# Layernorm, linear attention and a GELU layer on one core: W1 loaded as row blocks, tile 0 accumulated block by block

## The chip, the cores and the metric

One core of a Trainium2 chip runs the whole kernel in one launch. The metric is the device time of that launch in microseconds; before the change it was 204.91 us (median of 3 runs, 204.80 to 204.93). The profile of the kernel before has a span of 203.5 us from the first to the last instruction. Names: TensorE (PE in the profile, PEld for its weight loads, PEq for its sequencer), VectorE (DVE), ScalarE (ACT), GpSimd (POOL), SyncE (SP, which only issues transfers here).

## The reference, cut to what matters

```python
x = A_x                                   # [1, 2048, 640] bf16
xn = _layernorm(x, axis=-1)               # (x - mean) / sqrt(var + 1e-5)
return x + _A_ref(xn, A_wqkv, A_wo) + _B_ref(xn, B_w1, B_b1, B_w2, B_b2)

def _B_ref(x, w1, b1, w2, b2):            # w1 [640, 1536], w2 [1536, 640]
    h = _gelu(jnp.einsum("bsd,df->bsf", x, w1) + b1)
    return jnp.einsum("bsf,fd->bsd", h, w2) + b2
# _A_ref: linear attention with 32 heads of 20, phi(t) = where(t > 0, t + 1, exp(t)) + 1e-6
```

The change touches the start alone: the layernorm of the first tokens and h for them. The 2048 tokens are 16 tiles (t) of 128. D = 640 is five row blocks of 128 (k, DT = 5), F = 1536 is twelve column blocks of 128 (jb, JT = 12).

## The kernel before

A small planner notes for each instruction what it reads and writes, and puts in the semaphore waits; each engine runs its instructions in the order in which they are written here. `take(n)` gives the next of 8 PSUM banks in a ring. `HW` is half a row, 320 elements.

Loads, in order of issue: x tiles and W1 in three column thirds, of the first third two row blocks on ScalarE's queue.

```python
FW = F // NW1                                     # NW1 = 3, FW = 512
def dma_w1(i, eng="sync"):
    dma_w(eng, W1[:, :, i*FW:(i+1)*FW], w1v[:, :, i*FW:(i+1)*FW], r_W1[i])
KA = 2
dma_x(0, 1)
dma_w("scalar", b1tmp[:], B_b1..., r_b1tmp)
dma_w("scalar", W1[:, 0:KA, 0:FW], w1v[:, 0:KA, 0:FW], r_W1A)
dma_x(1, 1)
dma_w("sync", W1[:, KA:DT, 0:FW], w1v[:, KA:DT, 0:FW], r_W1[0])
dma_w1(1)
dma_x(2, 1)
dma_w1(2)
dma_x(3, 1); dma_x(4, 2); dma_x(6, 2); dma_x(8, 4)
```

Layernorm of a tile: two halves of statistics and their aggregate on VectorE (GpSimd adds eps in between), the power -0.5 on GpSimd, and the normalization on VectorE.

```python
def ln_half(t, h):      # VectorE bn_stats of half h; for h == 0 GpSimd then adds D*EPS
    ...
def ln_aggr(t):
    s = t % 4
    Pl.ins(v, lambda e: e.bn_aggr(aggr[:, s, :], stats[:, s, :]), ...)
    Pl.ins(g, lambda e: e.tensor_tensor(out=rstd[:, s:s+1], in0=aggr[:, s, 1:2],
                                        in1=mhalf[:], op=ALU.pow), ...)
def ln_stats(t): ln_half(t, 0); ln_half(t, 1); ln_aggr(t)
def ln_norm(t):         # VectorE tensor_scalar: (x - mean) * rstd, all 640 columns
    ...
```

h needs x with the feature on the partitions (xnT). Tiles 0 to 2 are transposed by TensorE into PSUM and copied from there, tiles 3 to 15 by a DMA transpose after their normalization. A unit of h is five matmuls and a Gelu:

```python
def h_unit(t0, n, jb):                            # n tiles at once
    b = take(1); w = n * P; tok = slice(t0*P, t0*P + w)
    Pl.ins("tensor", [matmul(bank(b, 0, w), W1[:, k, jb*P:(jb+1)*P], xnT[:, k, tok],
                             start=(k == 0), stop=(k == DT-1)) for k in range(DT)], ...)
    Pl.ins("scalar", ... HG[:, jb, tok] = Gelu(bank(b, 0, w) + b1c[:, jb:jb+1]))
```

The start of the schedule (shortened; `filler(n)` is n matmuls of 512 columns on zeros):

```python
... ScalarE: one Gelu on one column               # loads the Gelu table
filler(6); b1_step(); filler(3)
ln_stats(0); ln_half(1, 0); ln_half(1, 1)
norm_part(0, 0, CA, r_xnA); norm_part(0, CA, D, r_xnB)      # CA = 256 columns
ln_aggr(1)
dA, sA, bA = transp_part(0, 0, 2, r_xnA)
filler(1)
dB, sB, bB = transp_part(0, 2, DT, r_xnB)
... ScalarE copies part A to xnT, VectorE part B
norm_part(1, 0, CA, r_xnA1); norm_part(1, CA, D, r_xnB1)
h_first(0, [0, 1, 2, 3], r_xnTA, {... tile 1's transposes and copies in between})
h_first(1, [0, 1, 2, 3], r_xnTA1)                 # 40 matmuls of 128 columns
units(0, 2, JQ, 2*JQ + 1)                         # JQ = 4: 25 matmuls of 256 columns
ln_stats(2); ln_norm(2); ln_stats(3)
xnT_copy(2, transp(2))                            # VectorE copies tile 2's transposes
units(0, 2, 2*JQ + 1, JT)                         # 15 matmuls of 256 columns
ln_next(3)                    # ln_half(4, 0); ln_norm(3); ln_half(4, 1); ln_aggr(4)
xnT_dma(3)                                        # DMA transpose of tile 3
units(2, 1, 0, 10); units(3, 1, 0, 10); units(2, 2, 10, JT)
for t in range(4, NT): ...                        # layernorm and DMA transpose of the rest
```

Everything after this (the other h units, the attention, the output) is the same in both kernels.

Of the kernel before, what the change touches and what calls it, by code (L numbers as in the profile page):

```python
# [6 lines left out]
ACT = mybir.ActivationFunctionType  # L7
P = 128
FP32 = mybir.dt.float32
BF16 = mybir.dt.bfloat16  # L10
# [102 lines left out]
def bass_parallel_sum__linear_attn_block__dense_activation_gelu__prompt_kernel(  # L113
    nc: bass.Bass, A_x, A_wqkv, A_wo, B_x, B_w1, B_b1, B_w2, B_b2, out):
    Batch, S, D = A_x.shape
# [22 lines left out]
    with contextlib.ExitStack() as es:  # L138
# [59 lines left out]
        def take(n):  # L198
            b = ring[0]
            if n == 2 and b % 2:  # L200
                b += 1
            b %= 8
            ring[0] = (b + n) % 8
            return b

        def bank(b, lo=0, hi=512):
            return ps[:, b * 512 + lo: b * 512 + hi]
# [9 lines left out]
        r_xb = [R_("xb%d" % t) for t in range(NT)]  # L217
        r_xn = [R_("xn%d" % t) for t in range(NT)]
        r_xnT = [R_("xnT%d" % t) for t in range(NT)]
        NW1 = 3  # L220
        r_W1A = R_("W1_0A")
        r_W1 = [R_("W1_%d" % i) for i in range(NW1)]
        r_Wq, r_Wk, r_Wv, r_W2 = R_("Wq"), R_("Wk"), R_("Wv"), R_("W2")
        r_Wo = [R_("Wo%d" % i) for i in range(2)]
        r_oT = [R_("oT%d" % i) for i in range(2 * DT)]
# [31 lines left out]
        def dma_x(t, n):  # L257
            src = xv[t * P:(t + n) * P, :].rearrange("(t p) d -> p t d", p=P)
            Pl.ins("sync", lambda e: e.dma_start(x_in[:, t:t + n, :], src),
                   writes=r_x[t:t + n], dma=True)  # L260

        def dma_w(eng, dst, src, res):
            Pl.ins(eng, lambda e: e.dma_start(dst, src), writes=[res], dma=True)  # L263

        w1v = B_w1.rearrange("(k p) n -> p k n", p=P)
        wqv = A_wqkv.rearrange("(k p) n -> p k n", p=P)
        FW = F // NW1
        def dma_w1(i, eng="sync"):
            dma_w(eng, W1[:, :, i * FW:(i + 1) * FW], w1v[:, :, i * FW:(i + 1) * FW], r_W1[i])
        KA = 2  # L270
        dma_x(0, 1)
        dma_w("scalar", b1tmp[:], B_b1.rearrange("(a p) -> a p", p=P), r_b1tmp)
        dma_w("scalar", W1[:, 0:KA, 0:FW], w1v[:, 0:KA, 0:FW], r_W1A)
        dma_x(1, 1)
        dma_w("sync", W1[:, KA:DT, 0:FW], w1v[:, KA:DT, 0:FW], r_W1[0])
        dma_w1(1)
        dma_x(2, 1)
        dma_w1(2)
        dma_x(3, 1)
        dma_x(4, 2)  # L280
        dma_x(6, 2)
# [40 lines left out]
        def filler(n):  # L322
            b = take(1)
            Pl.ins("tensor", [lambda e: e.matmul(bank(b), warm[:, 0:P], warm[:], start=True, stop=True)
                              for _ in range(n)], reads=[r_warm], writes=[B_[b]])
# [9 lines left out]
        def ln_half(t, h):  # L335
            s = t % 4
            Pl.ins(v, lambda e: e.bn_stats(stats[:, s, 6 * h:6 * h + 6], x_in[:, t, h * HW:(h + 1) * HW]),  # L337
                   reads=[r_x[t]], writes=[r_stats[s][h]])
            if h == 0:
                Pl.ins(g, lambda e: e.tensor_single_scalar(stats[:, s, 2:3], stats[:, s, 2:3], D * EPS, ALU.add),  # L340
                       reads=[r_stats[s][0]], writes=[r_stats[s][0]])

        def ln_aggr(t):
            s = t % 4
            Pl.ins(v, lambda e: e.bn_aggr(aggr[:, s, :], stats[:, s, :]),
                   reads=r_stats[s], writes=[r_aggr[s]])
            Pl.ins(g, lambda e: e.tensor_tensor(out=rstd[:, s:s + 1], in0=aggr[:, s, 1:2],
                                                in1=mhalf[:], op=ALU.pow),
                   reads=[r_aggr[s], r_small], writes=[r_rstd[s]])

        def ln_stats(t):
            ln_half(t, 0)
            ln_half(t, 1)
            ln_aggr(t)
# [22 lines left out]
        def h_unit(t0, n, jb):  # L377
            b = take(1)
            w = n * P
            tok = slice(t0 * P, t0 * P + w)  # L380
            Pl.ins("tensor", [(lambda e, k=k: e.matmul(  # L381
                bank(b, 0, w), W1[:, k, jb * P:(jb + 1) * P], xnT[:, k, tok],
                start=(k == 0), stop=(k == DT - 1))) for k in range(DT)],
                reads=[r_W1[jb * P // FW]] + r_xnT[t0:t0 + n], writes=[B_[b]])
            Pl.ins("scalar", lambda e: e.activation(  # L385
                HG[:, jb, tok], bank(b, 0, w), ACT.Gelu_apprx_tanh, bias=b1c[:, jb:jb + 1]),
                reads=[B_[b], r_b1c], writes=[r_HG[t][jb] for t in range(t0, t0 + n)])


        CA = 2 * P  # L390
        r_xnA, r_xnB = R_("xn0A"), R_("xn0B")

        def norm_part(t, lo, hi, res):
            s = t % 4
            Pl.ins(v, lambda e: e.tensor_scalar(xn_tm[:, t, lo:hi], x_in[:, t, lo:hi], aggr[:, s, 0:1], rstd[:, s:s + 1],
                                                ALU.subtract, ALU.mult),
                   reads=[r_x[t], r_aggr[s], r_rstd[s]], writes=[res, r_xn[t]])

        def transp_part(t, k0, k1, res):
            b = take(1)  # L400
            pT = bank(b).bitcast(BF16)
            Pl.ins("tensor", [(lambda e, k=k: e.transpose(pT[:, (k - k0) * P:(k - k0 + 1) * P],
                                                          xn_tm[:, t, k * P:(k + 1) * P], ident[:]))
                              for k in range(k0, k1)],
                   reads=[res, r_ident], writes=[B_[b]])
            return xnT[:, k0:k1, t * P:(t + 1) * P], pT[:, 0:(k1 - k0) * P].rearrange("p (k q) -> p k q", k=k1 - k0), b

        def h_first(t, jbs, resA, between=None):
            bs = [take(1) for _ in jbs]
            tok = slice(t * P, (t + 1) * P)  # L410
            for (ks, res) in (((0, 1), resA), ((2, 3, 4), r_xnT[t])):
                for i, (jb, b) in enumerate(zip(jbs, bs)):
                    Pl.ins("tensor", [(lambda e, k=k, jb=jb, b=b: e.matmul(
                        bank(b, 0, P), W1[:, k, jb * P:(jb + 1) * P], xnT[:, k, tok],
                        start=(k == 0), stop=(k == DT - 1))) for k in ks],
                        reads=[r_W1A if res is resA else r_W1[jb * P // FW], res], writes=[B_[b]])
                    if between and res is not resA and i in between:
                        between[i]()
            for jb, b in zip(jbs, bs):
                Pl.ins("scalar", lambda e, jb=jb, b=b: e.activation(  # L420
                    HG[:, jb, tok], bank(b, 0, P), ACT.Gelu_apprx_tanh, bias=b1c[:, jb:jb + 1]),
                    reads=[B_[b], r_b1c], writes=[r_HG[t][jb]])

        r_xnTA, r_xnTA1 = R_("xnT0A"), R_("xnT1A")
        r_xnA1, r_xnB1 = R_("xn1A"), R_("xn1B")
        Pl.ins("scalar", lambda e: e.activation(b1c[:, 0:1], warm[:, 0:1], ACT.Gelu_apprx_tanh),
               reads=[r_warm], writes=[r_b1c])
        filler(6)
        b1_step()
        filler(3)  # L430
        ln_stats(0)
        ln_half(1, 0)
        ln_half(1, 1)
        norm_part(0, 0, CA, r_xnA)
        norm_part(0, CA, D, r_xnB)
        ln_aggr(1)
        dA, sA, bA = transp_part(0, 0, 2, r_xnA)
        filler(1)
        dB, sB, bB = transp_part(0, 2, DT, r_xnB)
        Pl.ins("scalar", lambda e: e.activation(dA, sA, ACT.Copy), reads=[B_[bA]], writes=[r_xnTA])  # L440
        Pl.ins(v, lambda e: e.tensor_copy(dB, sB), reads=[B_[bB]], writes=[r_xnT[0]])
        norm_part(1, 0, CA, r_xnA1)
        norm_part(1, CA, D, r_xnB1)

        def copy_part(k0, k1, res, dst):
            d, s, b = transp_part(1, k0, k1, res)
            Pl.ins(v, lambda e: e.tensor_copy(d, s), reads=[B_[b]], writes=[dst])

        h_first(0, [0, 1, 2, 3], r_xnTA, {1: lambda: copy_part(0, 2, r_xnA1, r_xnTA1),
                                          3: lambda: copy_part(2, DT, r_xnB1, r_xnT[1])})  # L450
        h_first(1, [0, 1, 2, 3], r_xnTA1)

        def xnT_dma(t):
            Pl.ins("sync", lambda e: e.dma_start_transpose(xnT[:, :, t * P:(t + 1) * P], xn_tm[:, t, :]),
# [1 line left out]

        late = Pl.records["sync"][x_done:]
        del Pl.records["sync"][x_done:]
        JQ = JT // NW1

        def units(t0, n, lo, hi):
            for jb in range(lo, hi):
                h_unit(t0, n, jb)

        def ln_next(t):
            if t + 1 < NT:
                ln_half(t + 1, 0)
            ln_norm(t)
            if t + 1 < NT:
                ln_half(t + 1, 1)  # L470
                ln_aggr(t + 1)

        units(0, 2, JQ, 2 * JQ + 1)
        ln_stats(2)
        ln_norm(2)
        ln_stats(3)
        xnT_copy(2, transp(2))
        units(0, 2, 2 * JQ + 1, JT)
        ln_next(3)
        xnT_dma(3)  # L480
        units(2, 1, 0, 10)
        units(3, 1, 0, 10)
# [353 lines left out]
```

## Time and profile before

| what | value |
|---|---|
| time, median of 3 | 204.91 us |
| span of the profile | 203.5 us, 3162 instructions |
| granted TensorE clock by the page | 1.00 |
| first row that uses W1 (L413) | starts at 6.45 us |
| tile 2's transposes on TensorE (L365) | start at 12.26 us |
| DMA transpose of tile 3, issue and length in the chain | 14.56 us, 2.66 us |
| first matmul on tile 3 | 17.27 us |
| last matmul ends, by the chain | 201.7 us |

How to read it: the page gives busy time by engine, the span in 40 slices of about 5 us (each digit is tenths of busy), and the chain of work that ended last, followed back from the last instruction. A row of the timeline has start, length, engine, line of the kernel, operation, destination and source, shapes and count, and in brackets how long the engine sat idle before it and what released it; instructions of one kind are merged. Matmuls are pipelined, so a merged length is more than the count times the spacing, and a row of "busy" on TensorE does not mean that it works at its peak. A transfer's time to landing runs from its issue to the semaphore's last step.

### The profile page before, as it was taken

The page shows a single profiled execution, that of the slowest core. Times are in us where ns is not written, and L with a number is a line of the kernel's source. Part 1 is how long each engine was busy: PE and PEld are TensorE (multiplying, and loading weights), DVE is VectorE, ACT ScalarE, POOL GpSimd, SP SyncE. Part 2 cuts the span into 40 slices and gives each one's busy share as a digit, 9 for nine tenths or more (in the row PEclk, how much of TensorE's full clock was granted, in tenths as well). Part 3 has the DMA queues.
Part 4 walks back from the last instruction along what each step waited for, and adds up shares of the span by engine and source line. Part 5 has one row for each costly group of instructions (what it writes and reads, how often), then busy time and mean ns, then how long its engine had stood idle before and what let it go on. Part 6 is the DMA issues. An engine that isn't in the chain of part 4 may idle for free.

```text
span 203.5 us, 3162 instructions
## 1 busy us (share of the span) xinstructions
PE 199.4 (98%) x1153; PEld 106.7 (52%) x1170; DVE 122.1 (60%) x246; ACT 73.6 (36%) x144; POOL 14.4 (7%) x43
## 2 busy tenths in 40 slices
PE   7999999999999999999999999999999999999996
PEld 2789885444444444644456565444444444444444
DVE  4579855000005899999458899595794297348222
ACT  3589886666667555121233596200000000000000
POOL 3136534000000000000000000000000000000000
PEclk9999999999999999999999999999999999999999
DMA  5974996999901111000179934117266926851541
GB/s 154 360 263 98 123 191 120 240 348 221 323 8 29 26 26 26 3 0 0 35 178 373 160 64 98 55 22 161 31 122 195 144 52 115 153 120 31 164 117 52
DMA packets 52550, 25.45 MB, mean 125 GB/s; under 512 B 38119, under 2 KB 52535, under 8 KB 52535
## 3 DMA queue, kind: packets, MB, share of 16 engines
q1 hardware_dynamic: 48782, 23.80, 50.1%
q10 hardware_dynamic: 3752, 1.45, 4.2%
q8 instruction: 9, 0.15, 0.3%
q14 instruction: 7, 0.05, 0.1%
HBM read 12.72 MB, written 2.62 MB: 75 GB/s over the span
## 4 chain that ended last, share of the span: by engine, by line
PE 90%; DMA 5%; DVE 2%; SPq 1%; issue 1%; POOL 0%; DVEq 0%
PE ps L745 29%; PE ps L381 21%; PE ps L584 11%; PE ps L573 8%; PE ps L532 8%; PE ps L710 7%; DMA xPK<-in_A_x_dram 3%; PE ps L563 2%; PE ps L523 2%; DMA xnT<-xn_tm 1%; DVE stats L337 1%; PE ps L598 1%; PE ps L616 1%; SPq L263 0%; DVE xn_tm L358 0%
## 5 line engine op out<-in xcount | busy, mean ns | idle before, releaser
L381 PE MATMUL ps<-xnT,W 128*128 128x256 bf16 (+2 forms) x372 | 50.5, 296 | 0.3
L385 ACT ACTIVATE HG<-ps,b1c 128x256 bf16<-128x256 f32 (+2 forms) x75 | 37.4, 522 | 13.5 <-PE ps L381 11.7
L745 PE MATMUL ps<-HG,W 128*128 128x512 bf16 x188 | 41.9, 379 | 0.2
L381 PEld LDWEIGHTS ps<-xnT,W 128*128 128x128 bf16 x375 | 32.2, 98 | 17.9 <-DMA xnT<-xn_tm 0.3
L745 PEld LDWEIGHTS ps<-HG,W 128*128 128x128 bf16 x192 | 18.8, 98 | 22.6
L584 PE MATMUL ps<-xnT,Wqkv 128*128 128x512 bf16 x97 | 22.4, 379 | 0.2
L745 PE MATMUL ps<-PQ,Msb 128*128 128x512 bf16 x78 | 17.8, 379 | 0.1
L532 PE MATMUL ps<-Wqkv,xnT 128*128 128x512 bf16 x78 | 17.8, 379 | 0.1
L573 PE MATMUL ps<-xPK,xn_tm 128*128 128x512 bf16 x78 | 17.2, 379 | 0.1
L337 DVE BATCH_NORM_STATS2 stats<-xPK 128x6 f32<-128x320 bf16 x32 | 13.7, 468 | 5.7 <-DMA xPK<-in_A_x_dram 5.7
L584 PEld LDWEIGHTS ps<-xnT,Wqkv 128*128 128x128 bf16 x100 | 11.3, 118 | 8.7
L507 ACT ACTIVATE xn_tm<-ps 128x512 bf16<-128x512 f32 x20 | 11.9, 597 | 9.5 <-PE ps L584 8.9
L510 DVE SCALAR_TENSOR_TENSOR PQ<-ps,xn_tm 128x512 bf16<-128x512 f32 x20 | 13.8, 692 | 2.1
L507 ACT ACTIVATE ek<-ps 128x512 bf16<-128x512 f32 x20 | 11.8, 597 | 8.4 <-PE ps L532 6.4
L518 DVE CAST b2c<-out_l 128x5 f32<-128x5 bf16 x1 | 0.2, 172 | 23.2 <-DMA out_l<-b2bc 23.2
L649 DVE TENSOR_REDUCE den_sb<-xn_tm 128x128 f32<-128x512 f32 x4 | 4.1, 1037 | 16.1 <-DMA xn_tm<-xn_tm 16.1
L751 DVE SCALAR_TENSOR_TENSOR W<-ps,b2c,xnT 128x512 bf16<-128x512 f32 x16 | 11.3, 734 | 2.8 <-PE ps L745 2.4
L532 PEld LDWEIGHTS ps<-Wqkv,xnT 128*128 128x128 bf16 x80 | 7.8, 98 | 9.4
L745 PEld LDWEIGHTS ps<-PQ,Msb 128*128 128x128 bf16 x80 | 7.8, 98 | 9.4
L573 PEld LDWEIGHTS ps<-xPK,xn_tm 128*128 128x128 bf16 x80 | 7.8, 98 | 9.3
L633 DVE SCALAR_TENSOR_TENSOR xn_tm<-PQ,z_sb,xn_tm 128x512 f32<-128x512 bf16 x16 | 12.0, 749 | 0.4
L510 DVE SCALAR_TENSOR_TENSOR xPK<-ps,ek 128x512 bf16<-128x512 f32 x16 | 11.1, 692 | 1.7
(66 smaller groups left out, 151.3 us busy)
## 6 DMA issues: line engine op xcount, KB each, us to landing
xPK<-in_A_x_dram SPq DMA_DIRECT2D x5, 640.0 KB, 6.9
Wqkv<-in_A_wqkv_dram SPq DMA_DIRECT2D x3, 800.0 KB, 7.6
W<-in_B_w_dram SPq DMA_DIRECT2D x1, 1920.0 KB, 15.0
out_dram<-xPK SPq DMA_DIRECT2D x3, 640.0 KB, 3.5
W<-in_B_w_dram SPq DMA_DIRECT2D x2, 640.0 KB, 7.7
xPK<-in_A_x_dram SPq DMA_DIRECT2D x4, 320.0 KB, 6.6
xn_tm<-xn_tm ACTq DMA_DIRECT2D x12, 64.0 KB, 3.2
Wo<-in_A_wo_dram SPq DMA_DIRECT2D x1, 750.0 KB, 12.6
```

The costliest lines, as they stand in the source:

```text
L337: Pl.ins(v, lambda e: e.bn_stats(stats[:, s, 6 * h:6 * h + 6], x_in[:, t, h * HW:(h + 1) * HW]), reads=[r_x[t]], writes=[r_stats[s][h]])
L381: Pl.ins("tensor", [(lambda e, k=k: e.matmul(bank(b, 0, w), W1[:, k, jb * P:(jb + 1) * P], xnT[:, k, tok], start=(k == 0), stop=(k == DT - ...
L385: Pl.ins("scalar", lambda e: e.activation(HG[:, jb, tok], bank(b, 0, w), ACT.Gelu_apprx_tanh, bias=b1c[:, jb:jb + 1]), reads=[B_[b], r_b1c ...
L507: Pl.ins("scalar", lambda e: e.activation(et, src, ACT.Exp), reads=[B_[b]], writes=[re])
L510: Pl.ins(v, lambda e: e.scalar_tensor_tensor(out=dst, in0=src, scalar=0.0, in1=et, op0=ALU.max, op1=ALU.add), reads=[B_[b], re], writes=[r ...
L532: Pl.ins("tensor", [(lambda e, k=k, b=b, t=t: e.matmul(bank(b), xnT[:, k, t * P:(t + 1) * P], Wqkv[:, k, D:D + CW], start=(k == 0), stop=( ...
L573: Pl.ins("tensor", lambda e, t=t, b=b, f=f: e.matmul(bank(b), xn_tm[:, t, f * P:(f + 1) * P], PK[:, t, 0:CW], start=(t == 0), stop=(t == N ...
L584: Pl.ins("tensor", [(lambda e, k=k, j=j, b=b: e.matmul(bank(b), Wqkv[:, k, j:D:DT], xnT[:, k, cc], start=(k == 0), stop=(k == DT - 1))) fo ...
L633: Pl.ins(v, lambda e: e.scalar_tensor_tensor(out=yv[c % 2], in0=pq, scalar=z_sb[:, j:j + 1], in1=yv[c % 2], op0=ALU.mult, op1=ALU.add), re ...
L710: return lambda e: e.matmul(bank(b, 0, cs.stop - cs.start), l, r[:, cs], start=(i == 0), stop=(i == JT + DT - 1))
L745: Pl.ins("tensor", lambda e, l=l, r=r, i=i: e.matmul(bank(b), l, r, start=(i == 0), stop=(i == JT + DT - 1)), reads=rd, writes=[B_[b]], ma ...
L751: Pl.ins(v, lambda e: e.scalar_tensor_tensor(out=oT[o], in0=bank(b), scalar=b2c[:, nb:nb + 1], in1=xnT[:, nb, cc], op0=ALU.add, op1=ALU.ad ...
```

## The change

W1 is loaded as five row blocks (k) of 128 x 1536 in place of three column thirds, and tile 0's h for all twelve column blocks is accumulated block by block, as they land, in six PSUM banks that stay open. Two column blocks with two tiles of 128 tokens each fill a bank. Each of these banks is opened once by a matmul on zeros (`start=True`)[...]; all later matmuls only add. Tile 1 is then added bank by bank, and a Gelu over 256 columns takes tiles 0 and 1 together. x0 comes as two halves of its columns, so that its first half of statistics may start sooner; all loads of x and W1 are in SyncE's queue. For tile 0 the reciprocal square root is VectorE's reciprocal and ScalarE's square root instead of GpSimd's power; the table of the square root is loaded at the start, that of Gelu after it. Tile 0 is normalized and transposed in three pieces (blocks 0; 1 and 2; 3 and 4). Tile 2's transposes now stand after tile 1's fifth bank.

The diff, cut to its core:

```diff
-        FW = F // NW1
-        def dma_w1(i, eng="sync"): ...
-        dma_x(0, 1)
-        dma_w("scalar", b1tmp[:], ...)
-        dma_w("scalar", W1[:, 0:KA, 0:FW], w1v[:, 0:KA, 0:FW], r_W1A)
-        dma_x(1, 1)
-        dma_w("sync", W1[:, KA:DT, 0:FW], w1v[:, KA:DT, 0:FW], r_W1[0])
-        dma_w1(1)
+        def dma_w1(k):
+            dma_w("sync", W1[:, k, :], w1v[:, k, :], r_W1[k])
+        for h in range(2):
+            dma_w("sync", x_in[:, 0, h*HW:(h+1)*HW], xv[0:P, h*HW:(h+1)*HW], r_x0[h])
+        dma_w1(0)
+        dma_x(1, 1)
+        for k in range(1, DT):
+            dma_w1(k)
         dma_x(2, 1)
-        dma_w1(2)
         dma_x(3, 1)
 ...
+            if t == 0:        # in ln_aggr
+                Pl.ins(v, lambda e: e.reciprocal(rstd[:, s:s+1], aggr[:, s, 1:2]), ...)
+                Pl.ins("scalar", lambda e: e.activation(rstd[:, s:s+1], rstd[:, s:s+1], ACT.Sqrt), ...)
+                return
 ...
+        def acc(jb, t):
+            lo = (jb % 2) * 2 * P + t * P
+            return bank(jb // 2, lo, lo + P)
+        def pass_k(k, res, jbs):      # one block k of tile 0, start=False, stop=False
+            for jb in jbs: ... matmul(acc(jb, 0), W1[:, k, jb*P:(jb+1)*P], xnT[:, k, 0:P])
+        def bank_1(i):                # tile 1 into bank i: 10 matmuls, then two Gelus of 256 columns
+            ...
+        ... ScalarE: activation Sqrt on one column; then the load of b1
+        filler(3)
+        for i in range(NB):           # NB = 6: open the banks
+            ... matmul(bank(i), warm[:, 0:P], warm[:], start=True, stop=False)
+        ln_stats(0)
+        ... ScalarE: activation Gelu on one column
+        for i, (k0, k1) in enumerate(pieces):      # ((0, 1), (1, 3), (3, 5))
+            norm_part(0, k0*P, k1*P, ...)
+        turn_0(0)                     # transpose, then copy: VectorE for piece 0, ScalarE for 1 and 2
+        turn_0(1)
+        ln_stats(1)
+        norm_part(1, 0, D, [r_xn[1]])
+        pass_k(0, kres[0], range(4))
+        turn_0(2)
+        pass_k(0, kres[0], range(4, JT))
+        pass_k(1, kres[1], range(JT))
+        b1_step()
+        for k in range(2, 4): pass_k(k, kres[k], range(JT))
+        ... tile 1 transposed and copied: blocks 0, 1 by VectorE, 2 to 4 by ScalarE
+        pass_k(4, kres[4], range(JT))
+        ln_half(2, 0); ln_half(2, 1); ln_aggr(2); ln_half(3, 0); ln_half(3, 1)
+        ln_norm(2); ln_aggr(3)
+        for i in range(NB):
+            bank_1(i)
+            if i == NB - 2:
+                ring[0] = 7
+                xnT_copy(2, transp(2))
+        ring[0] = NB
 ...
-        units(0, 2, JQ, 2*JQ + 1)
-        ln_stats(2); ln_norm(2); ln_stats(3)
-        xnT_copy(2, transp(2))
-        units(0, 2, 2*JQ + 1, JT)
-        ln_next(3)
+        ln_half(4, 0); ln_norm(3); ln_half(4, 1); ln_aggr(4)
         xnT_dma(3)
         units(2, 1, 0, 10)
```

## The prediction

> **What bounds the kernel now.** I read the page first: busy time and the 40 slices.
>
> ```profile
> PE 199.4 (98%) x1153; PEld 106.7 (52%) x1170; DVE 122.1 (60%) x246; ACT 73.6 (36%) x144; POOL 14.4 (7%) x43
> PE   7999999999999999999999999999999999999996
> ```
>
> TensorE has a row almost all the time, so a change to the first 15 us can only give what TensorE loses there. Where it loses it, the chain that ended last tells (start, length, what):
>
> ```profile
> 2.73 7.05 DMA xPK<-in_A_x_dram
> 9.80 0.90 DVE stats L337 x2
> ...
> 12.21 0.82 DVE stats L337 x2
> ...
> 13.33 0.35 DVE xnT L373
> 13.68 0.41 DVE stats L337
> 14.09 0.44 DVE xn_tm L358
> 14.56 2.66 DMA xnT<-xn_tm
> 17.27 13.92 PE ps L381 x150
> ```
>
> The early chain is not TensorE's. It is tile 2 of x landing at 9.8, VectorE's layernorm of tiles 2 and 3, and the DMA transpose of tile 3, for which TensorE waits until 17.27; from there it is TensorE to the end. So **the number to predict is the moment tile 3's first matmul starts, 17.27 now**; what follows (184.4 us to the last matmul) is untouched by the diff. Third, the timeline of TensorE up to there:
>
> ```profile
> 1.25 2.74 PE L324 MATMUL ps<-warm 128*128 128x512 bf16 x6 [1.25 <-DVE warm L294]
> 4.05 1.46 PE L324 MATMUL ps<-warm 128*128 128x512 bf16 x3
> 5.49 0.39 PE L402 MATMUL ps<-ident,xn_tm 128*128 128x128 bf16 x2
> ...
> 6.45 1.22 PE L413 MATMUL ps<-xnT,W 128*128 128x128 bf16 x14
> ...
> 8.16 1.42 PE L413 MATMUL ps<-xnT,W 128*128 128x128 bf16 x20
> 9.41 3.00 PE L381 MATMUL ps<-xnT,W 128*128 128x256 bf16 x25
> 12.26 0.45 PE L365 MATMUL ps<-ident,xn_tm 128*128 128x128 bf16 x5
> ```
>
> Useful work starts at 6.45. In the trace's own starts the spacing of matmuls is 0.427 us per 512 columns and 0.107 per 128 until 6.74, and 0.056 per 128, 0.109 per 256 after. From 6.45 to tile 2's transposes at 12.26 the gaps add up to only about 0.5 us. Last, the DMA view of the first 25 us (KB, median us from issue to landing):
>
> ```profile
> W<-in_B_w_dram SPq DMA_DIRECT2D x1, 384.0 KB, 5.4
> W<-in_B_w_dram ACTq DMA_DIRECT2D x1, 256.0 KB, 4.9
> ```
>
> W1's first two row blocks (ScalarE's queue) land at 6.4, when the first matmul starts; the rest of the first column third at 7.1, the second third at 9.3, the last at 11.7.
>
> **What the Trainium skill says.** "DMA: Bandwidth & Descriptors", section "Issuing engines are not separate DMA queues": queues of different engines share the same 16 DMA engines. The trace agrees: with both at work the 16 engines' share is 1.03 in 4.5 to 6.5 us. "Perfetto Trace Analysis", section "What "DMA-bound" means": where descriptor generation binds, large descriptors matter. The stages view fits: 196 GB/s at a share of 0.74 in 3.0 to 4.5 us, 375 GB/s at 1.08 in 6.5 to 9.0. "ScalarE: Activation LUTs", section "What ACT_TABLE_LOAD costs": 1283 ns a load plus a drain of about 1380 ns. The trace has the 1283 ns but no drain: the load starts at 1.95, its activation at 3.24. "TensorE: Matmul & The Clock Gate", section "What's actually happening": the clock is half until a busy window of about 3.4 us, free-running, has passed; the doubling of pace at 6.74, 5.5 us after the first matmul, agrees.
>
> **The change part by part.**
>
> (1) *Tile 0's statistics.* x0 (160 KB) landed at 3.10. I estimate the first half at 2.75 and the second, issued 0.47 later, at 3.0. Statistics then start near 2.78 instead of 3.12, the second 0.41 later (as now), and the aggregate 0.58 after that, at about 3.78 instead of 4.12.
>
> (2) *Square root.* Before, aggregate start to first normalize was 5.08 - 4.12 = 0.96 (GpSimd's power alone 0.57). Now a VectorE reciprocal (0.17, from the 128x5 cast) with its wait, about 0.27 from aggregate to reciprocal, 0.25 to ScalarE, 0.20 for a 128x1 activation (the 0.203 of L426) and 0.1 back: 0.83. First normalize at 4.6. The second table load runs from about 4.5 to 5.8 behind it; ScalarE's first copy of xnT then ends near 6.4, its second near 6.8. Both are before TensorE asks for them (7.1 and 8.5 below), so the load should cost nothing.
>
> (3) *TensorE's start.* Nine 512-column matmuls (three fillers, six that open the banks) take 9 x 0.427 from 1.25: free at 5.09. The first transpose follows at once. Its copy sits on VectorE behind all three normalize pieces (4.6, 4.95, 5.3, each 0.3 to 0.35), so it starts at 5.65; first useful matmul at about 5.95: **0.5 us earlier** than 6.45.
>
> (4) *W1 by rows.* A block is 128 rows of 3 KB, 384 KB. The packet records give 46 ns for 1 KB and 55 for 1.25 KB, so about 118 for 3 KB and 0.95 us for the eight rows of each DMA engine. With a first packet at about 2.9 and 0.4 for x1 (128 rows of 1.25 KB) in between, I estimate the blocks landed at 4.3, 5.9, 6.9, 7.8 and 8.8, and x2 at 9.2.
>
> (5) *TensorE's sum until tile 2's transposes.* From 5.95: eight instructions at the half clock (0.107) to 6.8; then 42 matmuls (rest of block 0, blocks 1 to 3) at 0.056, 2.35; b1, 0.05; five transposes of tile 1, 0.28; block 4, 0.67: 10.15. ScalarE's copy of tile 1's last three blocks allows bank 0 at 10.2. Five banks of ten matmuls, 50 x 0.056 = 2.8: 13.0. Tile 2's transposes, and VectorE's copy of them at **13.5**; before it started at 13.24. The reason is order, not speed: before, these transposes stood behind 40 matmuls of 128 and 25 of 256 columns (4.97 us of work), now behind 110 of 128 (6.16 us). The 1.2 us more eats the 0.5 us of the early start and the 0.5 us of gaps.
>
> (6) *Tile 3.* Behind that copy VectorE has one half of tile 4's statistics and tile 3's normalize, then the DMA transpose. Before: copy 13.24, normalize 14.09 (it waited for GpSimd's power of tile 3, done just before 14.0), transpose issued 14.56, first matmul 17.27. Now tile 3's power is long done (tile 3 lands before 10), so the normalize comes 0.72 after the copy: 14.2; transpose at 14.7; first matmul 14.7 + 2.71 = **17.4**. TensorE itself would be ready at 14.0 + 50 x 0.056 = 16.8 and waits 0.6 us.
>
> (7) *ScalarE.* Tiles 0 and 1 now get 12 Gelus of 256 columns (0.36 apart when nothing holds them: 0.26 for 128 columns, four in 1.14, plus 0.106, the difference of the means) after bank 0 is full near 11: 4.3 us, to 15.4. The ninth tile-2 unit takes bank 6 again near 16.3, after its Gelu at 15.7. Beside the path.
>
> Sum: 17.4 - 17.27 = +0.13 us, so 205.0; I add 0.1 for landings and clock, which can mostly err one way: **205.1 us**.
>
> **Rivals.**
> W1 binds. If blocks land by bytes as before (960 KB at 7.1, 1600 at 9.3, 2400 at 11.7), the last block, 2240 KB into the queue, comes at 11.2. Block 4, five banks and the transposes then put tile 2's copy at 15.2 and tile 3 near 19.1: 206.8 us. For it stand the measured landings; against it the starved early stage, which had 384 to 640 small rows per transfer where there are now 128 long ones.
>
> The clock stays low. Between 5.5 and 5.95 TensorE now idles, and the window is free-running; a further half-speed window to about 10.1 leaves out some 30 matmuls, +1.7 us: 206.7.
>
> TensorE's early start pays. If the clock rises by 4.7 and the copies come sooner, tile 2's transposes come 0.5 to 0.8 earlier and tile 3 moves to 16.8, where TensorE is ready anyway: 204.4. Nothing but tile 3 blocks it.
>
> ScalarE binds, if Gelus keep the 0.54 spacing now seen (2.11 us for 4): 12 x 0.54 = 6.5 us, to 17.6, and banks 6 and 7 come free late; about +1 us. Against: that spacing is five matmuls of 0.109, TensorE's pace.
>
> **Range and chances.** All of this moves one start by at most -0.9 to +1.9 us in 205. The range is 204.2 to 206.8, longer upwards, because both waits that could appear, block 4 and the clock, cost time. 2% is 4.1 us, twice the worst rival: within 2% at 0.96, slower 0.03, faster 0.01.
>
> **What the profile after would show.** First normalize at 4.6 and first W1 matmul at 5.95 (steps 1 to 3); W1 landings of 2.5 to 5 us after issue and no wait on W (step 4); tile 2's copy at 13.5 with VectorE idle before it (step 5); a wait of about 0.6 us for the transposed tile 3, ending near 17.4 (step 6); no wait for a Gelu (step 7). The prediction fails if the chain's early part runs through W instead of tile 3, if the 0.107 spacing lasts past 7, or if tile 3's normalize does not follow tile 2's copy.

## The result and the profile after

The changed kernel takes **206.75 us** (median of 4 runs, 206.32 to 207.15) beside 204.86 us of the kernel before on the same chip: a ratio of 1.0093, 95% interval 1.0072 to 1.0114. It is slower by 1.9 us. The span of the profile is 205.2 us, 1.7 more than before. From the page after, sections 1 and 2:

```profile
PE 199.8 (97%) x1192; PEld 107.9 (53%) x1209; DVE 122.3 (60%) x246; ACT 74.4 (36%) x145; POOL 13.7 (7%) x42
PE   7899999999999999999999999999999999999996
```

Busy shares tell nothing of the loss: TensorE is counted as busy as before. The chain that ended last does (start, length, what; the chain of the kernel after, rows of little length left out):

```profile
3.62 5.90 DMA W<-in_B_w_dram
9.56 0.84 PE ps L425 x12
...
11.46 2.85 PE ps L432 x50
14.31 0.29 PE ps L366 x5
...
15.04 0.48 DVE stats L333
15.52 0.35 DVE xn_tm L359
15.89 2.67 DMA xnT<-xn_tm
18.61 4.06 PE ps L382 x60
22.94 9.98 PE ps L382 x90
32.98 10.74 PE ps L382 x49
```

Two things are to be seen. The early part now begins with a W1 block (issued at 3.62, landed at 9.52), goes through TensorE's sums for tiles 0 and 1 (L425, L432) and tile 2's transposes (L366), and only then enters the VectorE and DMA-transpose steps of tile 3. Tile 3's first matmul stands at 18.61 instead of 17.27: **1.34 us**. And between 18.61 + 4.06 = 22.67 and 22.94 there is a second hole (0.44 us by the single starts). The stretch of 512 columns begins at 32.98, where it began at 31.24 in the chain of the kernel before:

```profile
31.24 10.74 PE ps L381 x49
```

That is 1.73 us, the whole difference of the spans, so the remaining **0.39 us** arise between the two.

The timeline of TensorE after, up to there (in brackets: idle before it, and what ended that):

```profile
5.79 0.58 PE L425 MATMUL ps<-xnT,W 128*128 128x128 bf16 x4 [0.20 <-DVE xnT L415]
...
6.38 1.72 PE L425 MATMUL ps<-xnT,W 128*128 128x128 bf16 x20
...
8.60 1.80 PE L425 MATMUL ps<-xnT,W 128*128 128x128 bf16 x24 [0.39 <-DMA W<-in_B_w_dram]
...
14.15 0.44 PE L366 MATMUL ps<-ident,xn_tm 128*128 128x128 bf16 x5
...
18.61 4.06 PE L382 MATMUL ps<-xnT,W 128*128 128x128 bf16 x60 [0.47 <-DMA xnT<-xn_tm]
22.94 11.28 PE L382 MATMUL ps<-xnT,W 128*128 128x256 bf16 x95 [0.27 <-issue]
```

The useful work starts 0.66 us earlier than before (5.79 for 6.45) and is then held up. At 8.60 the row names W1; inside the merged row there is one more hole. By the single starts, the time of the matmul before taken off, TensorE stood 0.46 us before block 2 and 0.28 us before block 3, 0.74 in all. The spacing of its matmuls fell from 0.107 to 0.056 us at 7.24 (6.74 before).

The DMA view of the first 25 us after, and the view by windows of 1 us (busy time by engine, granted clock, DMA share, GB/s):

```profile
W<-in_B_w_dram SPq DMA_DIRECT2D x5, 384.0 KB, 5.4
...
2.50:3.50 1.00, 1.00 (x4) 0.44 (x3) 0.71 (x2) 0.00 (x0) 0.13 (x1) 1.00 0.96 126
...
4.50:5.50 1.00, 1.00 (x5) 0.31 (x3) 0.90 (x4) 1.00 (x1) 0.00 (x0) 1.00 1.10 400
5.50:6.50 1.00, 0.80 (x9) 0.74 (x9) 0.98 (x3) 0.73 (x3) 0.21 (x1) 1.00 1.02 240
...
7.50:8.50 1.00, 0.71 (x12) 0.52 (x9) 0.45 (x1) 0.18 (x1) 0.01 (x1) 1.00 0.99 387
```

The five blocks landed at 5.20, 7.10, 8.56, 9.52 and 10.57. In 2.5 to 3.5 the 16 DMA engines were 0.96 busy and moved 126 GB/s, in 5.5 to 6.5 they were 1.02 busy and moved 240; elsewhere from 2.5 to 8.5 326 to 400, at a share of 0.86 to 1.10. The same two windows of the kernel before:

```profile
2.50:3.50 1.00, 1.00 (x4) 0.30 (x2) 0.38 (x1) 0.94 (x2) 0.00 (x0) 1.00 0.96 255
5.50:6.50 1.00, 1.00 (x8) 0.65 (x8) 0.46 (x2) 0.38 (x1) 0.46 (x1) 1.00 1.04 337
```

A busy DMA engine is thus no sign of a fast one, just as with TensorE.

### The profile page after: what moved, and what is told of

The parts are those of the page before. It is cut to its first block, busy times and chain, and to the rows that moved or that the text cites. A ratio compares the mean times of both kernels' runs of the same rounds, so it can differ in the third digit from the quotient of the medians.

```text
span 205.2 us, 3246 instructions
## 1 busy us (share of the span) xinstructions
PE 199.8 (97%) x1192; PEld 107.9 (53%) x1209; DVE 122.3 (60%) x246; ACT 74.4 (36%) x145; POOL 13.7 (7%) x42
## 3 DMA queue, kind: packets, MB, share of 16 engines
q10 hardware_dynamic: 3480, 1.18, 2.6%
## 4 chain that ended last, share of the span: by engine, by line
PE 92%; DMA 4%; SPq 1%; issue 1%; DVE 1%
PE ps L769 28%; PE ps L382 21%; PE ps L608 10%; PE ps L556 8%; PE ps L597 8%; PE ps L734 7%; DMA W<-in_B_w_dram 3%; PE ps L587 2%; PE ps L547 2%; PE ps L432 1%; DMA xnT<-xn_tm 1%; SPq L262 1%; PE ps L425 1%; PE ps L622 1%; PE ps L640 1%
## 5 line engine op out<-in xcount | busy, mean ns | idle before, releaser
L382 PE MATMUL ps<-xnT,W 128*128 128x512 bf16 (+2 forms) x332 | 46.0, 299 | 0.9 <-DMA xnT<-xn_tm 0.5
L386 ACT ACTIVATE HG<-ps,b1c 128x512 bf16<-128x512 f32 (+2 forms) x67 | 33.6, 546 | 12.8 <-PE ps L382 11.5
L382 PEld LDWEIGHTS ps<-xnT,W 128*128 128x128 bf16 x335 | 28.4, 98 | 18.2 <-DMA xnT<-xn_tm 0.6
L575 DVE TENSOR_TENSOR Msb<-Msb,xPK 128x640 f32<-128x640 f32 x14 | 11.6, 826 | 0.5
```

Source lines behind the costliest of these rows:

```text
L382: Pl.ins("tensor", [(lambda e, k=k: e.matmul(bank(b, 0, w), W1[:, k, jb * P:(jb + 1) * P], xnT[:, k, tok], start=(k == 0), stop=(k == DT - ...
L386: Pl.ins("scalar", lambda e: e.activation(HG[:, jb, tok], bank(b, 0, w), ACT.Gelu_apprx_tanh, bias=b1c[:, jb:jb + 1]), reads=[B_[b], r_b1c ...
```

## The experiments

Each is compared with the kernel before on the same chip. "Landed" is the last step of a transfer's semaphore. Four theories stood at first. **Landing**: W1's blocks come late, and TensorE's order passes that on to tile 2's transposes and tile 3. **Order**: there is more TensorE work ahead of tile 2's transposes, whatever lands. **Clock**: the hole before the first W1 matmul delays the rise of the pace. **Statistics**: the new square root or the halves of x0 cost something by themselves.

**1. Half of W1's bytes** (the changed kernel; columns 768 to 1535 of W1 are not loaded, and their products are formed from the first half's weights; TensorE's work is the same).

```diff
-  dma_w("sync", W1[:, k, :], w1v[:, k, :], r_W1[k])
+  dma_w("sync", W1[:, k, 0:F//2], w1v[:, k, 0:F//2], r_W1[k])
   # all matmuls of tiles 0 and up: weights jb -> jb % 6
```

> The changed kernel, but of each W1 row block only the first 768 columns are loaded, and column blocks 6 to 11 use the weights of blocks 0 to 5 (half of W1's bytes are left out, the output is another one; TensorE's instructions are the same in number and shape). If late landings are the cause (first theory): the blocks land near 4.4, 5.6, 6.4, 7.2 and 7.8 us instead of 5.2, 7.1, 8.6, 9.5 and 10.6, TensorE waits for none of them after 6, tile 2's copy comes at 13.7 instead of 14.63, tile 3's first matmul near 17.7 instead of 18.61, and the time falls by 0.9 to 1.3 us, to about 205.6. If the order is the cause (rival: tile 3 stands behind tile 2's copy, that behind 110 matmuls), the landings move and the time stays within 0.3 us of 206.75.

Measured: 205.57 us (205.18 to 207.42, 12 runs), ratio 1.0042 (1.0024 to 1.0061), 1.18 us below the changed kernel. The blocks landed at 4.22, 6.56, 7.05, 7.57 and 8.06. Its timeline of TensorE:

```profile
7.76 1.51 PE L425 MATMUL ps<-xnT,W 128*128 128x128 bf16 x24
...
13.02 0.44 PE L366 MATMUL ps<-ident,xn_tm 128*128 128x128 bf16 x5
...
17.46 4.06 PE L382 MATMUL ps<-xnT,W 128*128 128x128 bf16 x60 [0.46 <-DMA xnT<-xn_tm]
21.71 12.57 PE L382 MATMUL ps<-xnT,W 128*128 128x256 bf16 x102 [0.19 <-issue]
```

The row that began at 8.60 with a wait for W1 begins at 7.76 without one. Tile 2's copy is at 13.49 and tile 3's first matmul at 17.46: the course that the prediction had drawn (13.5 and 17.4). So the landing of W1 makes 18.61 - 17.46 = 1.15 us of the loss, the pace included: in this run it rose at 6.49. What is left in the span is 0.5 us (204.0 for 203.5): 0.19 at tile 3 and the rest in the hole before 21.71, which is in this kernel too. With fewer bytes ahead of it x2 lands earlier as well (8.49 for 11.03), and the transposes at 13.02 need that. In the changed kernel, though, tile 2 was normalized by 13.46 and its transposes began at 14.15, so x2 was not what held them there.

**2. Tile 3's normalize before tile 2's copy on VectorE** (the changed kernel).

```diff
   ln_norm(2); ln_aggr(3)
+  ln_half(4, 0); ln_norm(3)
   for i in range(NB): ...          # holds tile 2's copy
-  ln_half(4, 0); ln_norm(3)
   ln_half(4, 1); ln_aggr(4)
```

> The changed kernel with tile 3's normalization (and one half of tile 4's statistics) ahead of tile 2's copy in VectorE's order; loads and TensorE's order unchanged. If the order holds tile 3 back (rival of e1): the normalize starts at about 14.3 instead of 15.44, the transposed tile 3 is there at 17.5, before TensorE ends its 50 matmuls on tile 2 near 18.1, the wait of 0.68 us before tile 3 is gone and the time falls by 0.5 to 0.6 us to 206.2. If only the landings count (TensorE would be late by itself), the time stays within 0.2 us.

Measured: 206.55 us (205.98 to 208.6, 4 runs), ratio 1.0105 (1.0051 to 1.016). The chain of this kernel:

```profile
15.46 6.85 PE ps L382 x110
22.36 39.12 PE ps L382 x225
```

The wait for tile 3 is gone: transposed at 17.69, before it was needed, and TensorE runs from 15.46 on. The hole before tiles 4 and 5 shrinks from 0.44 to 0.21 us (tile 5's transpose landed at 22.27, their first unit began at 22.36). Yet the profiled run gained only 0.6 us of span. In that run the blocks landed at 5.13, 7.27, 8.81, 9.79 and 10.80 and tile 2's units began 0.28 us later than in the changed kernel (15.46 for 15.18). The intervals of the two kernels overlap. Tile 3's wait is the last link, not the source: without it TensorE itself is late, and the span is still 1.16 us over that of the kernel before.

**3. A filler in TensorE's hole before the first W1 matmul** (the changed kernel with one matmul of 512 columns on zeros more).

```diff
   turn_0(1)
+  matmul(bank(5), warm[:, 0:P], warm[:], start=False, stop=False)
```

> The changed kernel with one more 512-column matmul on zeros (added to an open bank, which it leaves as it is) in TensorE's idle 0.4 us before the first matmul with W1. If that gap delays the rise of TensorE's clock: the 0.107 us spacing ends near 6.7 instead of 7.3 and the next wait for W1 gets longer by as much, so that at most 0.2 us are gained: 206.6. If the rise follows a window of its own: no change of the time beyond 0.2 us, and the rise lies anywhere.

Measured: 206.58 us (206.52 to 206.66, 4 runs), ratio 1.0089 (1.0074 to 1.0104). The pace doubled at 7.09, against 7.24 without the filler, and the time is the same. Filling this hole gains nothing. A single trace of each cannot show more, because the moment of the doubling differs widely among the traces; what it is worth is seen in experiment 9. The blocks landed at 5.04, 6.96, 8.87, 9.82 and 10.84, and tile 3's first matmul came at 18.90.

**4. The statistics part alone** (the kernel before with x0 in two halves and ScalarE's square root for tile 0; W1 still in column thirds, the first piece in ScalarE's queue).

```diff
-  dma_x(0, 1)
+  for h in range(2):
+      dma_w("sync", x_in[:, 0, h*HW:(h+1)*HW], xv[0:P, h*HW:(h+1)*HW], r_x0[h])
   # ln_aggr(0): reciprocal on VectorE, Sqrt on ScalarE, then the Gelu table
```

> The kernel before with one part of the change alone: x0 in two halves, and VectorE's reciprocal with ScalarE's square root (and its two table loads) for tile 0. W1's thirds and all orders stay. By the reading that tile 3 bounds the start, this moves the first normalize from 5.08 to 4.5 and nothing after 9.8: 204.7 to 205.1, the same as before within 0.2 us. If TensorE's first matmul bounded it, up to 0.5 us faster; if the second table load stood in the way of ScalarE's first copy, up to 0.3 slower.

Measured: 206.47 us (12 runs, 205.12 to 206.89), ratio 1.0061 (1.0038 to 1.0085). That missed. Its chain:

```profile
1.27 2.92 DMA xPK<-in_A_x_dram
...
6.44 0.40 PE ps L411 x2
```

The first half of x0 landed at 2.84, but the second, issued at 1.27, only at 4.19. At 3.10 the whole x0 had been there before. W1's first piece, in ScalarE's queue from 1.49, landed at 4.78 instead of 6.39: it went ahead of half of x0. The first transpose is at 6.44 instead of 5.49, and the pace doubled only at 10.67: 31 instructions of 128 columns from 7.40 on ran at 0.107 instead of 0.056, some 1.6 us. Four of the twelve runs lie at 205.12 to 205.37 and the other eight at 206.37 to 206.89; only one of the eight was profiled. In the changed kernel, where nothing else is in ScalarE's queue but 3 KB of b1, the second half landed at 3.19.

**5. Tile 1's sums while W1 arrives** (the changed kernel; blocks 0 to 2 of tile 1 are added before blocks 3 and 4 are needed, and these two serve both tiles at once with 256 columns; block 4 is loaded after x2; tile 3's normalize directly follows tile 2's copy).

```diff
-  dma_w1(4); dma_x(2, 1)
+  dma_x(2, 1); dma_w1(4)
-  for k in range(2, 4): pass_k(k, kres[k], range(JT))
-  pass_k(4, kres[4], range(JT))
+  pass_k(2, kres[2], range(JT))
+  for k in range(3): pass_k(k, ..., range(JT), t=1)
   # bank_1: k in (3, 4), 256 columns; tile 2's transposes after bank 3
```

> The changed kernel with its remaining work laid out for the measured landings: tile 1's sums over blocks 0 to 2 are run while blocks 3 and 4 are still on their way, blocks 3 and 4 are then added for both tiles at once (256 columns) bank by bank; x2 is loaded ahead of block 4, and tile 2's transposes and tile 3's normalize come two banks earlier. Nothing is left out. If waits for blocks plus the order behind them are the whole of the loss: no wait for W1 but about 0.2 us near 8.4, units on tile 2 start near 14.2 (15.18 in the changed kernel, 14.19 before), tile 3 near 17.0 (18.61 and 17.27), and the time is 204.3 to 204.9, level with the kernel before or just under it. If the low clock at the start or ScalarE's Gelus are what counts, it stays above 205.5.

Measured: 206.38 us (four runs: 205.31, 206.11, 206.65, 206.96), ratio 1.0079 (1.0049 to 1.0108). Missed, though the profiled run is the one at 205.31. The chain of that run:

```profile
2.67 4.65 DMA W<-in_B_w_dram
...
12.09 4.51 ACT HG L439 x12
16.60 0.14 issue
16.73 43.84 PE ps L383 x300
```

Block 1 landed at 7.32 and is the only one waited for (0.68 us by the single starts); tile 3 comes in time. But now ScalarE is on the chain: its twelve Gelus end at 16.60 and hold TensorE for 0.43 us by the single starts. The other three runs are 0.8 to 1.65 us above the profiled one, and what held them is not on record.

**6. Twelve units of tiles 2 and 3 apart in the kernel before**, so that TensorE has work until tile 3 is transposed.

```diff
-  units(2, 1, 0, 10); units(3, 1, 0, 10); units(2, 2, 10, JT)
+  units(2, 1, 0, JT); units(3, 1, 0, JT)
```

> The kernel before with only one thing changed: all 12 column blocks of tile 2, and then all 12 of tile 3, instead of 10 and 10 and two units for both. TensorE has 0.56 us more to do before it needs tile 3, so if the wait of 0.29 us for tile 3's transpose is the only thing lost there, it vanishes and the time falls by 0.2 to 0.3 us to 204.5; if the wait is hidden elsewhere, no change.

Measured: 204.74 us (204.4 to 205.22, 22 runs), ratio 0.999 (0.9981 to 0.9998). The wait for tile 3 is gone, and what it was worth is only about 0.1 us, with an interval that ends almost at 1.

**7. Each W1 block as two transfers of 768 columns** (the changed kernel), to see whether rows of 3 KB are what starts slowly.

```diff
-  dma_w("sync", W1[:, k, :], w1v[:, k, :], r_W1[k])
+  for h in range(2):
+      dma_w("sync", W1[:, k, h*F//2:(h+1)*F//2], w1v[:, k, h*F//2:(h+1)*F//2], r_W1[2*k + h])
```

> The changed kernel with each W1 row block loaded as two transfers of 768 columns (rows of 1.5 KB, ten transfers instead of five), same order, same bytes. If rows of 3 KB are what makes the first blocks late, the blocks land about 0.5 us earlier and the time falls by 0.4 to 0.8 us to about 206.1. If the memory or the start of the queue limits it, the landings and the time stay within 0.3 us of 206.75; with twice the issues on SyncE the last block may even come later.

Measured: 207.08 us (206.74 to 207.97, 4 runs), ratio 1.011 (1.0081 to 1.0138). Each block was complete at 4.76, 7.50, 8.54, 9.83 and 10.85. The first is 0.44 us earlier, the others are as late as before or later. Between 1.5 and 3 KB, the length of the rows is not the cause; what makes these loads slow at first stays open.

**8. The square root alone** (the kernel before, x0 whole, ScalarE's square root for tile 0; the diff is the last line of experiment 4).

> The kernel before with VectorE's reciprocal and ScalarE's square root for tile 0 (and the two table loads), but x0 in one piece. e4, with x0 in halves too, was 1.3 us slower than expected; in its profile x0's second half landed at 4.19 instead of 3.10. If the halves did that, this kernel has its first normalize near 4.9 and is at 204.7 to 205.1, level with before. If the square root or its table load did it, it is again near 206.3.

Measured: 204.65 us (204.52 to 206.2, 20 runs), ratio 0.9994 (0.9981 to 1.0007). The square root and its second table load cost nothing measurable, and gain nothing. The two kernels differ in the halves of x0 alone, so it is these halves, beside W1 in another queue, that cost experiment 4 its 1.8 us. How much of it is the later first transpose and how much the low pace to 10.67 is not separated: in this run's trace the pace doubled at 4.04 already.

At this point one suspicion was left: all kernels with the halves had runs far apart or late, so the halves might also hold W1 back in the changed kernel. The last four runs asked that.

**9. The changed kernel with x0 in one piece.**

```diff
-  for h in range(2): dma_w("sync", x_in[:, 0, h*HW:(h+1)*HW], ..., r_x0[h])
+  dma_x(0, 1)
```

> The changed kernel with one edit: x0 loaded in one piece (160 KB, 128 rows of 1.25 KB), the rest as it is. If the two halves (256 rows of 640 bytes ahead of W1 in the same queue) hold the first W1 blocks back and make the kernel's time vary, the blocks land some 0.2 to 0.4 us earlier than 5.2, 7.1, 8.6, 9.5, 10.6, and the time is about 206.2 with runs within 0.5 us of each other. If the halves only cost ScalarE's queue in the kernel before, and here are what they were meant to be, the statistics come 0.3 us later, the landings and tile 3's first matmul (18.6) stay, and the time stays at 206.5 to 206.8 with runs as far apart as before.

Measured: 206.49 us (206.31 to 206.69, 6 runs), ratio 1.0068 (1.0044 to 1.0093). The statistics come later, as they must (x0 landed at 3.07), the blocks landed at 4.41, 6.92, 8.44, 9.38 and 10.40, and tile 3's first matmul is at 18.46. Block 0 gained 0.8 us, block 1 0.2 and the rest 0.1 to 0.2. The interval overlaps the changed kernel's. Here the halves neither bring nor cost much: the start of 5.87 instead of 5.79 is all that the whole x0 loses. From its timeline of TensorE:

```profile
5.87 0.38 PE L423 MATMUL ps<-xnT,W 128*128 128x128 bf16 x4 [0.19 <-DVE xnT L413]
...
8.48 1.78 PE L423 MATMUL ps<-xnT,W 128*128 128x128 bf16 x24 [0.56 <-DMA W<-in_B_w_dram]
...
18.46 4.06 PE L380 MATMUL ps<-xnT,W 128*128 128x128 bf16 x60 [0.46 <-DMA xnT<-xn_tm]
```

This answers the clock theory. Here the pace had doubled before the first W1 matmul (four in 0.38 us, for 0.58 in the changed kernel), and TensorE only stood the longer: by the single starts 0.32, 0.63 and 0.26 us before blocks 1, 2 and 3, 1.2 us in all for 0.74. Tile 3's first matmul came only 0.15 us earlier.

**10. Experiment 5 with x0 in one piece.**

> The kernel in which tile 1's sums over blocks 0 to 2 run while the last two blocks arrive, with x0 in one piece. That kernel with x0 in halves had one run at 205.31 and the others 0.8 to 1.6 us above it. If the halves cause that, all runs are near 205.0 to 205.4 now. If W1's rows in one queue cause it, the runs stay between 205.3 and 207.

Measured: 206.04 us (204.95 to 208.82, 22 runs), ratio 1.0059 (1.0036 to 1.0082). Eight runs lie between 204.95 and 205.50, others up to 207.5 and above. That the halves make the runs differ is refuted: this kernel has none. In its profile block 1 landed at 7.57 and block 4 at 10.99.

**11. Experiment 2 with x0 in one piece.**

> The changed kernel with tile 3's normalize ahead of tile 2's copy and x0 in one piece. Tile 3's wait (0.68 us) is gone as in the run with halves, so what is left is TensorE's own lateness: 0.6 us of waits for blocks 2 to 4 and 1.2 us of more work ahead of tile 2. I expect 0.5 us less than the changed kernel with x0 in one piece; 205.7 if that one is at 206.2.

Measured: 206.43 us (205.84 to 207.28, 7 runs), ratio 1.0074 (1.0048 to 1.01). Not told apart from experiment 9; the 0.5 us that were expected below it are not there. The profiled run is the slowest of the seven (207.28): block 1 landed at 7.95, TensorE stood 1.34 us before it, and the granted clock fell to half from 7.86 to 11.28, so that about 30 matmuls ran at 0.107.

**12. Experiments 6 and 8 together**, in search of a version that beats both kernels.

> The kernel before with ScalarE's square root for tile 0 and twelve instead of ten units of tiles 2 and 3 apart, in search of a version that beats both. Each alone was at 204.65 and 204.74, beside 204.84. If both add up, 204.5; if TensorE's spare 0.1 us is one and the same, 204.65.

Measured: 204.63 us (204.54 to 205.03, 22 runs) beside 204.94, ratio 0.9988 (0.9977 to 0.9998). It has the lowest ratio of all, 0.1% below the kernel before, with an interval that ends almost at 1. Whether the two parts add up is not told apart at this size.

## Why the prediction was right or wrong

The time lay in the stated range and within 2%, as forecast; the central value was 1.65 us too low. By two of the three signs that it had named for itself the main line failed: the chain's early part runs through W, and the spacing of 0.107 lasted past 7 (to 7.24). That the time still lies in the range, just under its upper end, it owes to a rival. Step by step:

| step | predicted | measured |
|---|---|---|
| 1 statistics start, aggregate | 2.78, 3.78 | 2.79, 3.81 |
| 2 first normalize | 4.6 | 4.49 |
| 3 first W1 matmul | 5.95 | 5.79 |
| 4 W1 blocks landed | 4.3, 5.9, 6.9, 7.8, 8.8 | 5.20, 7.10, 8.56, 9.52, 10.57 |
| 4 waits for W1 | none | 0.46 and 0.28 |
| 5 pace doubles | 6.8 | 7.24 |
| 5 tile 2's copy | 13.5 | 14.63 |
| 6 wait for tile 3 | 0.6 | 0.63 by the single starts |
| 6 tile 3's first matmul | 17.4 | 18.61 |
| 7 twelve Gelus | 0.36 apart, beside the path | 12 in 4.48, beside the path |

**Steps 1 to 3 held**, the first normalize and the first matmul a little early. The table load costs nothing on the path, as step 2 said: 1.28 us from 4.47, and the next activation 0.02 us after it. "ScalarE: Activation LUTs", section "What ACT_TABLE_LOAD costs", adds a drain to the load; neither kernel shows one, and experiment 8 finds no time for it either.

**Step 4 is the step that failed.** "I estimate the blocks landed at 4.3, 5.9, 6.9, 7.8 and 8.8" took 0.95 us for each block from the packet times of smaller rows. That size is right in the steady state: blocks 3 and 4 landed 0.96 and 1.05 after the ones before. The first three did not: 1.90 (with x1 in between) and 1.46. In the packet records the 23 rows of 3 KB that began in 2.5 to 3.4 us took 0.60 us on the median, and of the 73 that began in 5.5 to 6.4 a quarter took more than 0.18, up to 0.79, against 0.121 for most others. The windows show that as 126 and 240 GB/s at a full share. The prediction blamed small rows for the slow early stage, leaning on "Perfetto Trace Analysis", section "What "DMA-bound" means", that large descriptors matter where descriptor generation binds. With long rows the stage is slow as well, and experiment 7, with rows of half the length, lands blocks 1 to 4 no earlier. Over 4.5 to 8.5 us the windows give 344 GB/s on the mean, against 357 in the kernel before: **the change brought W1 no faster.**

Which rival won? "W1 binds" gave 206.8 by scaling the old landings by bytes (last block 11.2, tile 3 near 19.1). Measured were 10.57, 18.61 and 206.75. The mechanism is that rival's, with the last landing three quarters of the way from the main estimate to its own, and the total came out alike only because of the second hole. The main text had set the measured landings aside for a theory of rows, and that was the wrong choice. Experiment 1 shows the converse: with landings about as early as step 4 wanted them (only block 1 was 0.7 later), steps 5 and 6 come out at 13.49 and 17.46.

**Step 5 was right in its reason and too low in its size.** More work ahead of tile 2's transposes was to eat the early start, and did (experiment 1). The added 1.13 us to 14.63 are mostly the two waits (0.74) and the later pace: from 6.8 to 7.24 some four matmuls ran at 0.107 instead of eight at 0.056, about 0.2. As the first matmul was 0.16 early, some 0.3 are left; they lie in four short gaps around b1's and tile 1's transposes (0.06 to 0.10 each), which the sum did not have. "The clock stays low" was a rival only to 10.1; it did not come here, but did in experiment 4's trace (to 10.67). With first matmuls all at 1.25, the pace doubles anywhere from 4.04 (experiment 8) to 10.67. In experiment 11's record the granted clock changes at 4.45, 7.86 and 11.28, 3.41 us apart; a free-running window, as the prediction has it, would fit that, but no run tests it.

**Step 6 held** as a mechanism: statistics of tile 4, normalize and transpose follow tile 2's copy, and the first matmul is 18.61 - 15.89 = 2.72 after the issue, for 2.71 assumed. But "what follows is untouched by the diff" was wrong by **0.39 us**. The transposes of tiles 4 and 5 are issued later too (17.81 and 19.13); they landed at 22.29 and 22.85, and TensorE, ready at 22.49, began their first unit at 22.94, right after tile 5's. The DMA view of the issues at 17.5 to 20 us of the kernel after, and at 15 to 22 us of the kernel before:

```profile
xnT<-xn_tm SPq DMA_TRANSPOSE x2, 4.1
```

```profile
xnT<-xn_tm SPq DMA_TRANSPOSE x5, 2.6
```

Tile 4's transpose took 4.5 us to landing in place of 2.6; by the single steps of its semaphore one of the 16 DMA engines was 1.9 us late. Tile 5's came behind it and took 3.7. A fetch of 16 KB of instructions runs from 20.00 for 1.19 us, while tile 4's transpose is on its way. The same coincidence is in all fourteen traces: a 16-KB fetch of 0.9 to 1.5 us begins somewhere from 19.06 to 22.80, a transpose that is then on its way is the first to take 4.2 us or more (up to 5.6), and all before that one took 2.55 to 2.67. In the kernel before the fetch begins at 21.50 and meets tile 7's transpose, for which TensorE does not yet wait. An earlier fetch, from about 14 us, ends before tile 3's issue or at most 0.8 us after it, and delays nothing. No run moved the fetch, so that it causes the delay is likely but not shown.

**Step 7 held.** ScalarE came onto the path only in experiments 5 and 10, when all else was earlier.

What stays open is why kernels of this kind differ so from run to run. Experiment 10 goes from 204.95 upwards by over 2 us, experiment 12 stays within 0.5 us. The landings of W1 differ from profile to profile (block 1 at 7.10, 7.27, 6.96, 7.32, 6.92, 7.57, 7.95 in the changed kernel and experiments 2, 3, 5, 9, 10, 11), and a schedule that waits for each block passes that on, but no profile of one kernel in both kinds of run exists to show it. The fall of the clock seen in experiment 11 leaves its mark in a run's mean granted clock, 0.992 there. Only four other runs on record have that value (208.6 in experiment 2, 206.89 in 4, 207.43 and 208.82 in 10), so it belongs to the upper end of the spread and does not explain the rest.

## What to carry to other kernels

To consume an operand block by block makes each block's landing a wait, and in the first 10 us of a kernel those landings are better taken by bytes from the kernel at hand than from packet times of a later, steady stage (for the last block 11.2 and 8.8, where 10.57 was measured). An earlier first matmul is worth nothing if the instruction that opens the critical chain (here tile 2's transposes) stands behind more work than before: count the work ahead of it in the engine's order, and follow all later transfers of the same kind, not the first alone. A load that is split to come sooner can lose its second half to a load of another queue.

## What the runs showed of the hardware

DMA engines at a share of 1.02 moved 240 GB/s in 5.5 to 6.5 us, and at 0.99 they moved 387 in 7.5 to 8.5, with the same rows of 3 KB. A split of x0's 160 KB put its second half at 4.19 us beside W1 in another queue, and at 3.19 us without it, where the whole had landed at 3.10 beside the same W1. The spacing of TensorE's matmuls halved anywhere from 4.04 to 10.67 us, though the first matmul is at 1.25 in every trace, and in one trace it doubled again for 3.4 us at the end of a stand of 1.34. And in every trace one DMA transpose took 4.2 to 5.6 us where those before it took 2.55 to 2.67, while a 16-KB fetch of instructions ran.
